# Two of VectorE's three power readings summed by accumulating DMAs in an attention and MLP kernel

## The chip, the cores and the metric

The kernel runs on one core of one Trainium2 chip. The core has five instruction queues: TensorE (PE in the profile; PEld are its weight loads), VectorE (DVE), ScalarE (ACT), GpSimd (POOL) and SyncE (SP), and 16 DMA engines that all queues share. The on-chip memories are SBUF and PSUM; PSUM has eight banks of 128 x 512 fp32. The metric is device time in microseconds, as the median of several runs; a profiled execution is recorded beside them.

## The reference

Two branches over the same 2048 tokens of width 640, mixed by a gate that is one number per token:

```python
qkv = (x @ wqkv).reshape(B, S, 3, H, Dh).transpose(2, 0, 3, 1, 4)   # S = 2048, H = 32, Dh = 20
scores = einsum("bhqd,bhkd->bhqk", q, k) * Dh ** -0.5
a = einsum("bhqk,bhkd->bhqd", softmax(scores), v).transpose(0, 2, 1, 3).reshape(B, S, D) @ wo

h = einsum("bsd,df->bsf", x, w1) + b1                             # F = 1536
b = einsum("bsf,fd->bsd", h * tanh(softplus(h)), w2)

g = sigmoid((x * gate_w).sum(-1, keepdims=True))
out = g * a + (1 - g) * b
```

Both branches read the same x. All matrices are bf16. The largest part is the softmax: 32 heads x 2048 x 2048 exponentials.

## The kernel before

**Groups, sets and units.** The attention is cut into 32 groups G: four heads (p) times 512 queries (qc). Within a group the 2048 keys are 16 blocks j of 128. The scores of one block and one head are a *unit*: 128 keys x 512 queries, one PSUM bank, one matmul with a 32-row tile (L1033, four heads in four row tiles). A whole block j of a group, four units, goes one of two ways:

- *ScalarE's way.* Steps S n,bank write n units into n neighbouring banks (`emit_s`); step x exponentiates them in one instruction into the ring E (`emit_exp`, L1051). Step V j,-1 multiplies the block with the values (`emit_pv`, L1068): four matmuls, one per head, 21 value columns each (20 and a column of ones, which gives the softmax's denominator), accumulated in bank 7.
- *VectorE's way, a "set".* Step d takes block j out of the group for VectorE and gives it a tile T of 128 x 2048 bf16. Steps D compute its four units, and for each a VectorE instruction (L556, `power_of`) multiplies and adds so that the result, taken as int16, is the bit pattern of a bf16 power of two with a linear mantissa. One such power is a coarse exponential. So further *readings* are made of it: GpSimd adds a constant to the bits (an INT64_ADD over the tile, L586, `add_shift`), which moves the place where the mantissa breaks, and the readings are added up.

**Readings before.** In 153 of 160 sets (`d_shifts`) there are three readings: T itself and two shifted copies, made by two INT64_ADDs (the last in place). All three go to TensorE: V j,0 with the values VA, V j,1 and V j,2 with values scaled by RATIO (VD, made per p by two VectorE instructions). That is three readings, 12 matmuls, for one set; the sum is made in PSUM. In 7 of 160 sets (`d_sum`) GpSimd shifts T into a second tile, VectorE adds T to it (L610), GpSimd then shifts T in place, and TensorE reads two tiles: the sum with VA, the shifted T with VD.

**The other work of the same engines.** Projections, the value matrix, the two MLP products and the output product are "chains": step C takes the next one with a bank, every step F runs one piece (four matmuls, L633), and at its end VectorE copies the bank out. VectorE also normalises each finished group (transpose L1097, reciprocal L1104, product L1111). ScalarE runs the MLP's activation in two long instructions (step m, L840). SyncE issues the loads and stores: per group four query rows (step q, L749), per p the keys (step k), stores of the normalised groups (L1144), the MLP's weights (L431) and its results.

**The order.** Nothing is scheduled while the kernel runs: every engine's queue follows `ORDER`, a recorded list of steps in order of time, that a loop runs through (`steps`). Step y n runs the n-th waiting VectorE instruction, p n,k the n-th waiting GpSimd step, with k the tile T that it may write (-1: in place). Each step appends to its engines' queues, which run in order; a wait in front of an instruction holds all that stands behind it on that engine. There are nine tags for tiles T (T0 to T8), 18 units in the ring E and seven banks for scores and chains. Step H is four matmuls with zero weights that keep TensorE busy.

Of the kernel before, what the change touches and what calls it, by code (L numbers as in the profile page):

```python
# [11 lines left out]
ALU = mybir.AluOpType  # L12
# [7 lines left out]
S2,0 S2,2 C1,6 F x C2,5 F y1 x C3,4 F y2 S2,0 y3 C4,6 F x S3,2 y4 C5,5 F F F F x F F F F F F F F F F F F S2,0  # L20
F F S3,2 x F F C0,6 F F y5 x y6 F y7 F y8 y9 F S2,0 y10 V0,-1 x V1,-1 V2,-1 C6,6 F F F F F V3,-1 C7,5 F y11
C8,4 F y12 S2,0 S2,2 q1 C9,6 F y13 x C10,5 F y14 C11,4 F F x F F y15 F S2,0 F F F F x F F F S2,2 F F F F x F
S2,0 S2,5 F F F x y16 C12,3 F y17 y18 F y19 F y20 F x S3,0 F V4,-1 x V5,-1 y21 V6,-1 C13,6 F S3,3 y22 C14,2 F
x S2,0 y23 C15,6 F C16,2 F x y24 S3,3 y25 V7,-1 C17,6 F x F F F F F F F F F S2,0 F F F F x F S3,2 F F F F F
C18,5 F x F y26 y27 F y28 S2,0 y29 y30 F F x S2,2 y31 V8,-1 V9,-1 x V10,-1 d1,0,1 S2,0 S2,4 d1,1,0 D1,15,0,6
d1,2,0 d1,3,0 x C19,3 F y32 F F F x S3,0 D1,15,3,6 F y33 V11,-1 x S2,4 y34 C20,6 F F F F F F F F F F F x F
S3,0 D1,14,0,3 F F F y35 F F x F F F S2,4 y36 C21,3 F y37 y38 F y39 y40 e0 F v0 y41 F x S3,0 D1,15,1,6 q2 y42
V12,-1 y43 F V13,-1 x V14,-1 y44 S2,4 D1,14,3,6 C22,3 F y45 F F x F S2,0 D1,15,2,2 V15,-1 y46 F x F F S2,4
D1,13,0,6 y47 F p1,4 F F x C23,2 F F y48 F S2,0 F y51 F x S2,4 D1,13,3,6 y52 F y49 F y50 F F F x V0,-1 S2,0
D1,14,1,3 V1,-1 y53 x p2,-1 V15,0 S2,4 y55 C24,6 F y56 x F y57 F S2,0 D1,14,2,2 y54 d1,4,0 F x S2,3 D1,12,0,5  # L30
y58 F V2,-1 y59 x V15,1 p3,5 S2,0 D1,13,1,2 y60 V3,-1 V14,0 x y61 p4,0 S2,3 D1,12,3,5 C25,6 V14,1 y62 F x S2,0
D1,13,2,2 d2,1,0 F y63 F x S3,3 F p5,5 F x V4,-1 S2,0 D1,12,2,2 y64 V14,2 V13,0 y65 V5,-1 p6,0 x V13,1 S3,3
D1,12,1,6 d2,5,0 V6,-1 y66 C26,2 F x F F V13,2 F S2,0 D1,11,0,6 p7,2 F F y67 F x F q3 S2,3 D1,11,1,5 p8,0
V12,0 y68 F F x S2,0 D1,11,3,6 V7,-1 y69 V12,1 y70 x V12,2 y71 S2,2 D1,11,2,5 D2,15,1,4 d2,0,0 V8,-1 y72 x
C27,6 F F S2,0 F y73 p9,2 F F x F S2,2 D2,15,2,5 F F y74 F p10,3 F x S2,0 D2,15,0,4 V11,0 y75 V9,-1 y76 x
V11,1 y77 S2,2 D2,14,1,6 D2,14,2,5 V11,2 y78 x V10,-1 S2,0 D2,15,3,4 d2,2,0 y80 C28,6 F x F S2,2 y79 V0,-1 x
y81 F S2,0 D2,14,0,5 F y82 p11,3 y83 F x S2,2 D2,13,1,4 V1,-1 y85 V15,0 p12,4 x S2,0 D2,14,3,5 y86 d2,6,0
V15,1 C29,6 F y87 x F S2,2 D2,13,2,4 V15,2 y84 F F x y88 p13,1 F S2,0 D2,13,0,5 F F y89 F x F S2,2 D2,12,1,4
p14,3 F V2,-1 y90 V14,0 x S2,0 D2,13,3,5 y91 d3,4,0 C30,4 F F y92 F x F y93 F S2,2 D2,12,2,6 F F y94 F x F
S2,0 D2,12,0,5 V3,-1 y95 F x V14,1 S2,2 D2,11,1,6 y96 p15,1 V14,2 y97 V4,-1 x y98 S2,0 D2,12,3,5 d3,3,0 V13,0  # L40
y99 V5,-1 x S3,2 D2,11,2,6 p16,-1 V13,1 y100 V6,-1 x V12,0 p17,1 S2,0 D2,11,0,5 V13,2 y101 C32,6 F F p18,0 x F
S3,2 D2,11,3,5 d3,5,0 F y102 x F V7,-1 V12,1 y103 S2,0 D3,15,1,5 p19,1 V12,2 y104 V8,-1 x S3,2 D3,15,0,6 V11,0
p20,0 y105 V11,1 x S2,0 D3,15,2,5 V9,-1 y106 C31,6 F F F x S3,2 D3,14,1,5 V11,2 y107 F x F S2,0 y108 V10,-1
C33,5 F F y109 x F S3,2 D3,14,2,6 F y110 y111 x F V0,-1 S2,0 y113 C34,6 F F F y112 F F x F S3,2 D3,15,3,5 q4
d3,0,0 F F y114 F x F V1,-1 V2,-1 y115 S2,0 D3,13,1,5 p21,1 y116 V15,0 y117 C35,6 F x F S3,2 k1 p22,2 F F F F
x F S2,0 D3,14,3,5 F F y118 F V15,1 V3,-1 x V15,2 y119 S3,2 D3,12,1,5 y120 V4,-1 v1 y121 C36,6 F x F F y122
# [36 lines left out]
S2,2 D8,13,1,6 x y261 V15,0 V2,-1 y262 V15,1 x p67,0 S2,0 D8,13,0,5 D8,13,3,4 V15,2 y259 y263 V3,-1 x V14,0
# [213 lines left out]
def kernel(  # L297
# [12 lines left out]
    nc = tc.nc  # L310
# [1030 lines left out]
```

## Time and profile before

| | |
|---|---|
| median of 3 runs | 697.11 us (696.96 to 699.27) |
| profiled execution, its own time | 697.02 us |
| its span, first to last instruction | 695.2 us |
| TensorE's granted clock | 0.998 |
| chain that ended last, shares | PE 78%, ACT 15%, DVE 3%, issue 3%, DMA 1% |
| L1068 on E, on T with VA, on T with VD | 133.9, 62.4, 117.4 us busy for 1408, 640, 1252 matmuls |
| DMA queue of SyncE and ScalarE (q1) | 38.38 MB, 24.7% of 16 engines' span |
| DMA, whole core | 40.46 MB, mean 58 GB/s |

The page gives for each engine how long it was busy, and for each group of instructions how long the engine stood idle before it and which engine's instruction ended that idle time. Matmuls overlap one another, so a TensorE that is busy is not necessarily at its peak, and a group's busy time is not the time that it would be shorter without it. DMA issues are not counted as busy time of the issuing engine.

### The profile page before, as it was taken

The page shows a single profiled execution, that of the slowest core. Times are in us where ns is not written, and L with a number is a line of the kernel's source. Part 1 is how long each engine was busy: PE and PEld are TensorE (multiplying, and loading weights), DVE is VectorE, ACT ScalarE, POOL GpSimd, SP SyncE. Part 2 cuts the span into 40 slices and gives each one's busy share as a digit, 9 for nine tenths or more (in the row PEclk, how much of TensorE's full clock was granted, in tenths as well). Part 3 has the DMA queues.
Part 4 walks back from the last instruction along what each step waited for, and adds up shares of the span by engine and source line. Part 5 has one row for each costly group of instructions (what it writes and reads, how often), then busy time and mean ns, then how long its engine had stood idle before and what let it go on. Part 6 is the DMA issues. An engine that isn't in the chain of part 4 may idle for free.

```text
span 695.2 us, 24441 instructions
## 1 busy us (share of the span) xinstructions
PE 680.5 (98%) x10325; PEld 240.0 (35%) x10325; DVE 582.0 (84%) x1009; ACT 676.6 (97%) x665; POOL 339.6 (49%) x334
## 2 busy tenths in 40 slices
PE   8999999999999999999999999999999999999997
PEld 4433333332323343333333222222234333343333
DVE  4488868888799888788898999988989988888896
ACT  5899999999999999999999999999999999999996
POOL 5025443435365434544547555554643565545543
PEclk9999999999999999999999999999999999999999
DMA  9612132313211212112031214232222121143221
GB/s 249 194 15 46 32 75 52 58 51 85 50 26 33 67 37 40 27 38 56 24 83 36 43 32 90 44 67 57 37 63 81 22 50 29 41 74 61 58 58 48
DMA packets 125613, 40.46 MB, mean 58 GB/s; under 512 B 91136, under 2 KB 124944, under 8 KB 125504
## 3 DMA queue, kind: packets, MB, share of 16 engines
q1 hardware_dynamic: 123904, 38.38, 24.7%
q8 instruction: 80, 1.31, 0.8%
q10 hardware_dynamic: 1600, 0.53, 0.3%
q14 instruction: 29, 0.24, 0.1%
HBM read 23.61 MB, written 12.79 MB: 52 GB/s over the span
## 4 chain that ended last, share of the span: by engine, by line
PE 78%; ACT 15%; DVE 3%; issue 3%; DMA 1%; SPq 0%; DVEq 0%; ACTq 0%
PE Sp L1033 26%; PE Sp L1068 26%; PE Sp L633 24%; ACT E L1051 11%; ACT big L840 3%; DVE T L556 2%; DMA w_top<-in_A_wqkv_dram 1%; PE Sp L1284 0%; ACT L1051 0%; PE Sp L1184 0%; DVE VD L538 0%; DVE big L819 0%; DVE T L1111 0%; PE Sp L643 0%; DVE bt L864 0%
## 5 line engine op out<-in xcount | busy, mean ns | idle before, releaser
L1051 ACT ACTIVATE E<-Sp 128x1024 bf16<-128x1024 f32 (+1 forms) x650 | 645.5, 1175 | 5.1 <-PE Sp L1033 4.0
L586 POOL INT64_ADD T<-T x320 | 330.4, 1043 | 340.6 <-DVE T L556 195.8
L556 DVE TENSOR_SCALAR T<-Sp 128x512 int16<-128x512 f32 x640 | 425.0, 685 | 76.9 <-PE Sp L1033 67.3
L1033 PE MATMUL Sp<-qT,kT 32*128 32x512 bf16 x2048 | 260.4, 383 | 6.2 <-ACT E L1051 3.0
L1033 PEld LDWEIGHTS <-kT 32*128 32x128 bf16 x2048 | 71.5, 91 | 240.5 <-issue 236.0
L1068 PE MATMUL Sp<-E,VA 128*21 128x512 bf16 x1408 | 133.9, 383 | 0.0
L1068 PE MATMUL Sp<-T,VD 128*21 128x512 bf16 x1252 | 117.4, 382 | 0.2
L633 PE MATMUL Sp<-w_sb,big 128*32 128x320 bf16 x1536 | 74.2, 301 | 0.6 <-DVE T L556 0.5
L633 PE MATMUL Sp<-xT,w1t 128*32 128x512 bf16 x960 | 73.4, 383 | 0.2
L1068 PEld LDWEIGHTS <-VA 128*21 128x21 bf16 x2048 | 45.5, 90 | 63.3 <-issue 54.2
L1068 PE MATMUL Sp<-T,VA 128*21 128x512 bf16 x640 | 62.4, 381 | 0.0
L633 PE MATMUL Sp<-xT,ws 128*32 128x512 bf16 x720 | 52.3, 381 | 0.2 <-ACT E L1051 0.2
L633 PEld LDWEIGHTS <-big 128*32 128x32 bf16 x1536 | 35.0, 95 | 28.0 <-issue 19.6
L1068 PEld LDWEIGHTS <-VD 128*21 128x21 bf16 x1252 | 30.8, 90 | 39.1 <-issue 32.7
L819 DVE TENSOR_SCALAR big<-Sp,b1f 128x512 bf16<-128x512 f32 x48 | 35.6, 741 | 1.5 <-PE Sp L633 1.1
L633 PE MATMUL Sp<-wv,xT 128*32 128x81 bf16 (+2 forms) x960 | 33.3, 257 | 0.4 <-DVE st L721 0.2
L633 PE MATMUL Sp<-wo_sb,od 128*32 128x320 bf16 (+1 forms) x608 | 28.9, 301 | 0.6 <-DVE T L556 0.6
L633 PEld LDWEIGHTS <-w1t 128*32 128x32 bf16 x960 | 20.1, 95 | 26.3 <-issue 19.4
L721 DVE CAST st<-Sp 128x512 bf16<-128x512 f32 x36 | 24.7, 685 | 5.3 <-PE Sp L633 5.2
L633 PEld LDWEIGHTS <-xT 128*32 128x32 bf16 x960 | 19.1, 96 | 12.8 <-issue 9.2
L777 DVE CAST VA<-Sp 128x80 bf16<-128x80 f32 (+2 forms) x48 | 16.2, 373 | 8.2 <-PE Sp L633 8.2
L633 PEld LDWEIGHTS <-ws 128*32 128x32 bf16 x720 | 16.8, 95 | 17.7 <-issue 10.0
(75 smaller groups left out, 206.1 us busy)
## 6 DMA issues: line engine op xcount, KB each, us to landing
w1t<-in_B_w_dram SPq DMA_DIRECT2D x24, 320.0 KB
q_dram<-st SPq DMA_DIRECT2D x20, 128.0 KB
b_dram<-bt SPq DMA_DIRECT2D x16, 160.0 KB
bl<-b_dram SPq DMA_DIRECT2D x16, 160.0 KB
out_dram<-ot SPq DMA_DIRECT2D x16, 160.0 KB
qT<-q_dram SPq DMA_DIRECT2D x124, 20.0 KB
o_dram<-T SPq DMA_DIRECT2D x120, 20.0 KB
kT<-k_dram SPq DMA_DIRECT2D x28, 80.0 KB
```

The source lines that it names most:

```text
L556: nc.vector.tensor_scalar(out=dst.bitcast(I16), in0=src, scalar1=inv_sqrt_dh * LOG2E * 128.0, scalar2=127.0 * 128.0 + (BETA2 if two else B ...
L586: nc.gpsimd.int64_add(dst[:, :].bitcast(I64), src[:, :].bitcast(I64), n * 0x0001000100010001)
L633: nc.tensor.matmul(out_[k : k + 32], lhsT=lhsT[:, k : k + 32], rhs=rhs, tile_position=(0, k), **kw)
L721: nc.vector.tensor_copy(out=res["st"][:, :], in_=ps[:, :])
L777: nc.vector.tensor_copy(out=VA[:, sts[i], h0 : h0 + nh, 0:DH], in_=ps[:, i, 0:n].rearrange("p (h d) -> p h d", d=DH),)
L819: nc.vector.tensor_scalar(out=big[:, pair_of(c, ft), (ft % 2) * QC : (ft % 2 + 1) * QC], in0=ps[:, :], scalar1=b1f[:, ft : ft + 1], scalar ...
L840: nc.scalar.activation(v, v, ACT.Mish)
L1033: nc.tensor.matmul(ps_cols, lhsT=kT[p][32 * t_ : 32 * t_ + 32, j * P : (j + 1) * P], rhs=qT[G][32 * t_ : 32 * t_ + 32, :], tile_position=( ...
L1051: nc.scalar.activation(E[:, x : x + n, :], allb[:, k0 : k0 + n, :], ACT.Exp, scale=inv_sqrt_dh,)
L1068: nc.tensor.matmul(acc[32 * t_ : 32 * t_ + DH + 1, :], lhsT=lhsT, rhs=rhs, start=(pv_done[G] == 0), stop=(pv_done[G] == pv_total[G] - 1), ...
```

## The change

`d_sum`'s sum is no longer a VectorE instruction. GpSimd issues a DMA instead, from T to the shifted tile, that adds to its destination; it is queued as one more GpSimd step, and the second shift follows as a step after it:

```diff
         def shift(k):
             d[0] = t_tile(k)
             add_shift(d[0], d["T"], SHIFT2[0])
-            dve(total, lambda: gps(again))
-
-        def total():
-            nc.vector.tensor_tensor(out=d[0][:, :], in0=d[0][:, :], in1=d["T"][:, :], op=ALU.add)
+            gps(total)
+
+        def total(k):
+            nc.gpsimd.dma_start(out=d[0][:, :], in_=d["T"][:, :], accum_op=ALU.add)
+            gps(again)
 
         def again(k):
             d[1] = d["T"]
             add_shift(d[1], d["T"], SHIFT2[1])
```

The DMA waits for the first shift; the second shift and the reading V j,0 wait for the DMA. In the order, p n,-2 is the step that issues it.

`ORDER` is replaced as a whole. What the two lists hold:

| steps | before | after |
|---|---|---|
| sets (d) | 160 | 172 |
| of them summed to two readings | 7 (by VectorE) | 151 (by DMA) |
| units on VectorE (D) | 640 | 688 |
| blocks of scores and exponentials (S, x) | 650 | 668 |
| of 1, 2, 3 units | 0, 542, 108 | 1, 642, 25 |
| units on ScalarE | 1408 | 1360 |
| readings (V): of E, first, second, third | 352, 160, 160, 153 | 340, 172, 172, 21 |
| readings in all | 825 | 705 |
| VectorE instructions by step y | 975 | 1016 |
| GpSimd steps p: shifts, DMA issues | 320, 0 | 344, 151 |
| chains, pieces (C, F) | 191, 1223 | 191, 1223 |
| heating (H) | 3 | 9 |
| loads q, k, b, o; m | 31, 7, 16, 8; 2 | 31, 7, 16, 8; 2 |

The order's texture changes with it. A stretch from before and one from after; the DMA issue p n,-2 stands between a set's first shift (p n,k) and its second (p n,-1), with other sets' steps between:

```diff
-y505 V12,0 x V13,1 y508 p152,2 S2,0 D16,11,2,6 d17,5,0 V3,-1 y509 C110,5 F p153,-1 F x F S3,2 D16,10,0,6 F
...
+x y550 p253,-1 V12,1 S2,2 D17,13,0,6 D17,13,3,5 V7,-1 x y551 S2,0 D17,14,2,4 p256,3 d17,4,1 V8,-1 y552 V11,1 x
+C113,6 F F y553 p258,-2 S2,2 D17,12,0,5 F x y554 S2,0 D17,13,1,4 p259,5 F y555 F x V9,-1 S2,2 D17,12,3,5 y556
+p261,-2 C114,4 F F x y557 S2,0 D17,13,2,6 d17,7,1 F p257,-1 y558 F x S2,2 D17,11,0,5 V10,0 y559 F x S2,0
```

More of the change, by code (lines that the diff above doesn't have):

```diff
@@ L25 @@
[L25 to L34, printed above, removed]
@@ L280 @@
[L280 to L283 removed]
+S2,0 S2,2 C1,6 F x C2,5 F y1 C3,4 F x y2 S2,0 C4,6 F y3 x S3,2 y4 C5,5 F F F F F x F F F F F F F F F F F F F F
@@ new lines @@
+d5,8,1 F x y176 F S2,2 D5,13,1,5 p62,-2 F y177 x V8,-1 S2,0 D5,13,0,4 p58,-1 V12,0 y178 C45,5 F x F F y179
+S2,2 D5,13,2,6 p63,7 F F x y180 S2,0 D5,13,3,4 V9,-1 y181 p65,-2 V12,1 x C46,6 F y182 S2,2 D5,12,1,5 d5,4,1 F
+p61,-1 y183 x F S2,0 D5,12,0,4 F y184 x F S2,2 D5,12,2,5 V11,0 y185 p64,-1 V10,-1 x S2,0 D5,12,3,4 y186 d5,2,1
+V11,1 C47,6 F y187 x S2,2 D5,11,1,5 p67,3 F y188 F x S2,0 D5,11,0,4 y189 p69,-2 F F y191 x V15,0 S2,2
+D5,11,2,5 p66,-1 y192 V14,0 x V0,-1 S2,0 D5,11,3,4 y193 d6,0,1 V15,1 p68,7 V1,-1 y194 x S2,2 D5,10,1,6
@@ new lines @@
+D5,10,2,5 V2,-1 y190 p72,5 y195 V14,1 x S2,0 D5,10,0,4 V3,-1 y196 C48,6 F p71,-2 x F y198 S2,2 D6,15,1,5 F
+y197 x F S2,0 D5,10,3,4 y199 p73,-2 d6,1,1 F x V4,-1 y200 S2,2 D6,15,2,5 V13,0 p70,-1 y201 V5,-1 x S2,0
+D6,15,0,4 y202 C50,6 F p76,3 F x F F y203 F S2,2 D6,14,1,5 V13,1 y204 p77,-2 x S2,0 D6,15,3,4 y205 d6,6,1
+C57,6 V6,-1 F y206 x F S2,2 D6,14,2,5 p74,-1 V12,0 y207 F x q7 S2,0 D6,14,0,4 q8 F p79,7 y208 F x S2,2
+D6,13,1,5 q9 V11,0 y209 p75,-1 V7,-1 x S2,0 D6,14,3,4 y210 d6,5,1 V12,1 p80,-2 V8,-1 y211 x V11,1 S2,2
@@ new lines @@
+V12,1 S2,2 D9,10,3,5 d10,1,0 C72,6 F p137,-1 y325 x V13,1 V6,-1 S2,0 D10,15,0,4 F p139,-2 y326 x S2,2
+D10,15,2,5 F y327 V12,2 p140,0 x F S2,0 D10,15,1,4 F y328 V7,-1 x p142,-2 S2,2 C73,5 F y329 F F x S2,0
+D10,14,0,4 F V8,-1 y330 x F S2,2 y331 D10,15,3,6 d10,3,1 C74,4 F x y332 F S2,0 D10,14,1,5 F p144,6 x y333
+V9,-1 S2,2 D10,14,2,6 F y334 x V11,0 p141,-1 S2,0 D10,13,0,5 F y335 C75,6 F x p145,-2 F S2,2 y336 D10,14,3,5
+d10,5,1 F x p143,-1 y337 S2,0 D10,13,1,4 F y338 x V10,0 S2,2 D10,13,2,5 F y339 V11,1 x S2,0 V10,1 y340 C77,5 F
@@ new lines @@
+x S2,2 D19,15,0,4 V13,2 y602 p285,7 F x S2,0 D19,15,2,5 k5 V5,-1 k6 y603 F x p284,-2 S2,2 D19,15,1,4 V6,-1
+y604 C122,5 F x F p286,-2 y605 S2,0 D19,15,3,6 v5 d19,0,1 F y607 x F S2,2 D19,14,0,4 y606 p283,-1 F V12,0 x
+y609 S2,0 D19,14,2,6 V7,-1 p289,3 y610 V12,1 x S2,2 D19,14,1,4 y611 V8,-1 p290,-2 C123,5 F x F y612 S2,0
+D19,14,3,6 d19,8,1 F y608 x F y613 S2,2 D19,13,0,4 p287,-1 F y614 x V11,0 S2,0 D19,13,2,6 V9,-1 y615 p288,-1
+V10,0 x S2,2 D19,13,1,4 y616 V11,1 p292,5 C124,5 F y617 x S2,0 D19,13,3,6 d19,2,1 V10,1 y618 F x S2,2
@@ new lines @@
+S2,2 D21,14,1,5 q24 V7,-1 y675 x V11,0 S2,0 D21,14,3,6 p319,-1 y676 d21,6,0 V8,-1 C132,4 F x y677 S2,2
+D21,13,0,5 F y678 F x p325,7 S2,0 D21,13,2,6 F y679 F x p321,-1 S2,2 D21,13,1,5 V10,0 y680 V9,-1 x S2,0
+D21,13,3,6 y681 p326,-2 d21,8,0 V11,1 V10,1 y682 x C133,5 F S2,2 D21,12,0,4 y683 d22,0,0 F p328,2 x F y684
+S2,0 D21,12,2,6 F p324,-1 y685 V15,0 x y686 S2,2 D21,12,1,4 d22,4,0 V0,-1 y687 V1,-1 x S2,0 D21,12,3,6 y688
+p329,-2 F V2,-1 x y689 S2,2 D21,11,0,4 V15,1 y690 V3,-1 x C134,6 F S2,0 y691 D21,11,1,5 p327,-1 V14,0 x y692
@@ new lines @@
+V15,0 C152,6 F x y816 p387,-1 F S2,2 F y817 V14,0 x S2,0 D25,10,3,5 p388,-1 F V2,-1 y818 x V15,1 S2,2
+D25,11,2,4 p391,5 d26,0,1 F V3,-1 y819 x S2,0 D26,15,0,5 p390,-1 V13,0 y820 b5 V14,1 x y821 C155,4 F S2,2
+D25,10,1,6 p392,-2 F F y822 o1,0,4 x F S2,0 D26,15,3,5 F p393,1 V4,-1 y823 x V13,1 S2,2 D25,10,2,6 y824
+d26,3,1 C153,5 F p395,-2 F y825 x F F S2,0 D26,14,0,4 F V5,-1 p397,6 y826 x S2,2 D26,15,1,6 F V6,-1 y827 x F
+S2,0 D26,14,3,4 p398,-2 F F y828 x F S2,2 D26,15,2,6 d26,7,1 F V7,-1 y829 x F p394,-1 S2,0 D26,13,0,4 y830
@@ new lines @@
+p441,-1 F F y914 x F S2,2 D29,15,3,5 p446,-2 d29,0,1 F F y915 F x S2,0 D29,14,1,6 F F y916 F x F S2,2
+D29,14,0,5 y917 V12,0 V6,-1 x y918 S2,0 D29,14,2,6 D29,13,1,4 p448,2 V12,1 y919 V11,0 x S2,2 D29,14,3,5
+p444,-1 d29,3,1 V7,-1 y920 V8,-1 x D29,13,0,6 y921 S2,0 D29,13,2,4 p449,-2 V9,-1 y922 x V11,1 S2,2 D29,13,3,5
+y923 p450,5 d29,7,1 C172,6 F F x V10,0 y924 S2,0 D29,12,1,4 F p447,-1 F y925 x F S2,2 D29,12,0,5 y926 b10
+C173,4 F p452,-2 F x y927 F S2,0 D29,12,2,6 V10,1 p453,6 y928 x F S2,2 D29,12,3,5 d30,8,1 F y929 F F x F
@@ new lines @@
+p455,-2 S2,0 D29,11,1,6 y930 V0,-1 F y932 x S2,2 D29,11,0,5 p451,-1 F y931 F y933 F x V15,0 S2,0 D29,11,2,6
+y935 p457,2 V1,-1 y934 x V2,-1 S2,2 D29,11,3,5 D30,15,0,4 V3,-1 V15,1 x y936 p458,-2 S2,0 d30,4,1 V14,0 y937
+V4,-1 x S2,2 D30,15,3,6 p454,-1 y938 C176,5 F F x F F y939 S2,0 D30,15,1,4 p460,5 F F y940 x F F S2,2
+D30,14,0,6 p456,-1 F F x y941 S2,0 D30,15,2,4 F p461,-2 F y942 V13,0 x o2,4,5 o3,0,3 S2,2 D30,14,3,6 y943
+d30,6,1 V5,-1 V14,1 y944 x S2,0 D30,14,1,5 D30,14,2,4 p463,1 V6,-1 y945 V12,0 x V13,1 S2,2 D30,13,0,6 y946
@@ L284 @@
+V3,-1 x p488,-1 S2,2 D31,10,3,6 y1001 V14,1 y1002 C186,4 F x S2,0 D31,10,1,5 p489,1 F y1000 F F x F S2,2
+D31,9,0,6 y1003 p490,2 V4,-1 V12,1 y1004 x S2,0 D31,10,2,5 y1005 p491,3 V11,0 V12,2 x S2,2 D31,9,3,4 y1006
+V5,-1 y1007 V11,1 p492,0 x V11,2 S2,0 D31,9,1,6 D31,9,2,5 V6,-1 y1008 x V10,0 p493,1 V10,1 S2,2 y1009 C187,6 F
+F x F F p494,0 S1,0 y1010 V7,-1 x V10,2 V9,0 p495,2 V9,1 V8,-1 C188,6 F F F F C189,5 F V9,2 y1011 F F F y1012
+C190,4 F F F F y1013 y1014 y1015 y1016
 """
```

485 lines of the change are left out of this document (232 added, 253 removed).

## The prediction

> **What bounds the kernel now.** I read the header first, then the busy time by stages, then the groups of instructions kept apart by shape, then single pieces of the timeline. The header (PE is TensorE, PEld its weight loads, DVE VectorE, ACT ScalarE, POOL GpSimd):
>
> ```profile
> span 695.2 us, 24441 instructions
> PE 680.5 (98%) x10325; PEld 240.0 (35%) x10325; DVE 582.0 (84%) x1009; ACT 676.6 (97%) x665; POOL 339.6 (49%) x334
> ```
>
> Two engines at 97 and 98% of a mean over unequal stages; so the stages (columns: start:end, length, busy us of PE, PEld, DVE, ACT, POOL with instructions, then TensorE's clock, DMA share, GB/s):
>
> ```profile
> 0.00:25.00 25.00, 20.88 (x344) 11.42 (x348) 11.12 (x42) 16.05 (x18) 9.23 (x14) 1.00 0.97 257
> 300.00:400.00 100.00, 99.86 (x1483) 32.45 (x1483) 87.52 (x145) 99.93 (x102) 55.46 (x54) 1.00 0.20 45
> 400.00:500.00 100.00, 99.66 (x1316) 28.35 (x1316) 90.68 (x152) 99.93 (x104) 55.12 (x55) 1.00 0.27 57
> ```
>
> From 300 to 500 us ScalarE is never idle (99.93) and TensorE hardly ever; VectorE has 9 to 12 us in 100 free, GpSimd 45. So two engines set the pace together, and a gain needs less work on both. The groups (last columns: busy us, mean ns of one, idle before them):
>
> ```profile
> L1051 ACT ACTIVATE E<-Sp 128x1024 bf16<-128x1024 f32 x542 | 521.6, 1102 | 4.6 <-PE Sp L1033 3.7 <-ACT E L1051 0.2
> L556 DVE TENSOR_SCALAR T<-Sp 128x512 int16<-128x512 f32 x640 | 425.0, 685 | 76.9 <-PE Sp L1033 67.3 <-POOL T L586 1.3 <-issue 0.2
> L586 POOL INT64_ADD T<-T x320 | 330.4, 1043 | 340.6 <-DVE T L556 195.8 <-PE Sp L1068 62.9 <-PE Sp L1033 33.6
> L1051 ACT ACTIVATE E<-Sp 128x1536 bf16<-128x1536 f32 x108 | 166.6, 1543 | 0.5 <-PE Sp L1033 0.4
> ...
> L610 DVE TENSOR_TENSOR T<-T 128x2048 bf16<-128x2048 bf16 x7 | 8.5, 1207 | 0.6 <-POOL T L586 0.6
> ```
>
> The exponentials (L1051) are 645.5 us of ScalarE's 676.6 (the two shapes overlap, so their busy times add to more). GpSimd waits for work: 340.6 us idle before its shifts. TensorE's true price of one reading, four matmuls of L1068, is the distance between starts, 0.22 us, since the matmuls overlap:
>
> ```profile
> 676.72 0.40 PE L1068 MATMUL Sp<-T,VD 128*21 128x512 bf16 x4
> ...
> 676.94 0.39 PE L1068 MATMUL Sp<-E,VA 128*21 128x512 bf16 x4
> ...
> 677.16 0.31 PE L633 MATMUL Sp<-wo_sb,od 128*32 128x320 bf16 x4
> ```
>
> **The change part by part.** Counts are from the two recorded orders.
>
> *ScalarE.* Score units of 512 columns exponentiated fall from 1408 to 1360, in 668 instructions (642 of two units, 25 of three, 1 of one) for 650 (542 and 108). Three units last 1543 - 1102 = 441 ns longer than two. With a for the two-unit step, 542a + 108(a + 0.441) = 645.5 gives a = 0.920 us. After: 642 x 0.920 + 25 x 1.361 + 0.48 = 625.1. Saved: 20.4 us, on the path.
>
> *TensorE.* Readings fall from 825 to 705: 120 x 0.22 = 26.4 us less. Heating steps rise from 3 to 9 (1.3 us), and 18 more blocks of scores each switch the shape once more; a block of three or four scores takes 0.32 to 0.33 us in the chain of waits against 0.22 for a reading, so about 0.11 each, 2 us. Net 23 us less, a little more than ScalarE saves: TensorE does not become the bound.
>
> *VectorE.* 48 more powers (688 for 640) at 425.0/640 = 0.664 us are 31.9 us; the seven sums of L610 go, 8.5. So 582.0 + 23.4 = 605.4, 90% of a 675 us span. In dense stages it is nearly full: in the order's stretch that answers to 400 to 500 us the powers rise from 106 to 114, and 90.7 + 5.3 = 96 us stand in a stage shortened to about 97.
>
> *GpSimd.* Two INT64_ADD a set for 172 sets: 344 for 320, 25 us more. New are 151 DMA issues. No row shows one. Below: SyncE's issue rows, median 482 ns for the stores of o_dram; above: twice an INT64_ADD, 2.08 us. I take one INT64_ADD, 1.04: the row nearest in engine and operand size, and between the two ends. Then 339.6 + 25 + 157 = 522 us, 77% of the span. A set costs 2.08 + 1.04 = 3.1 us against one set in about 3.7 (172 sets in some 640 us): it fits, with 0.6 to spare.
>
> *The accumulating DMA's time.* It replaces a wait inside the engines by one on a transfer of 128 x 2048 x 2 B = 524 KB. Behind it waits GpSimd's own second shift (it overwrites the source), and behind that, in GpSimd's order, the next sets' shifts and issues; TensorE's reading V j,0 waits for the same DMA. From the rows: in the first 25 us the DMA engines were 97% busy at 257 GB/s, so one pass of 524 KB is 2.04 us, two passes (source and destination both read) 4.08. The fixed part: the last store of 160 KB is issued by
>
> ```profile
> 691.86 0.89 SPq L1310 DMA_DIRECT2D out_dram<-ot  x2
> ```
>
> so by 692.75, and the span ends at 695.2: 2.45 us, less 0.64 for the bytes, 1.8. Lower end 1.8 + 2.04 = 3.8 us; upper end 1.8 + 4.08 stretched by the other queue's 24.7% share, 1.8 + 5.4 = 7.2; the issue comes on top. The order puts 6 to 8 exponentials between issue and second shift in 146 of 151 sets (most often 7), at 625.1/668 = 0.94 us or more: 6.6 us. The first reading stands behind 6 or more too. Up to 7.2 + 1.04 = 8.2 against 6.6: most of the interval is covered. I take 5.5 us with issue, near the middle, where nothing waits.
>
> [...]
>
> *SyncE's queue.* Its loads and stores keep their kinds and counts; the order leads each group's query load by 10 or more exponentials (before, two stood at 1 and 4), which covers a load delayed by a summing DMA. Cost nothing; without that cover, one 0.5 to 3 us stall for each of 31 loads. Tiles T stay longer in use (a source is held for about seven exponentials more), all within the nine tiles; a late DMA also frees them late, and then VectorE's next power, its bank, and TensorE's next score are late.
>
> *Sum.* The profiled execution took 697.02 us, 1.8 outside its span, and the median is 697.11. 697.0 - 20.4 = 676.6. After the last exponential the order has 5 readings and 12 pieces of product where it had 3 and 6; two readings (0.4) and six pieces at about 0.17 make 1.4 us more tail. **678 us.**
>
> **The rivals.**
>
> *Slower: the DMAs set the pace.* Up to three are in flight: from one issue to the third after it lie its completion and three INT64_ADD on GpSimd, so three sets take at least L + 3.1 us, where the order wants 3 x 3.7 = 11.1. L up to 8.0 is free; beyond it each microsecond costs 151/3 = 50 us. At L = 8.4 the gain is gone; at 9, 151 x (12.1/3 - 3.7) = 50 us: 728. For it: three in flight share the same engines with 24.7% of other traffic, and if each kept the engines busy for 4.08 us, 151 x 4.08 + 172 = 788 us of DMA time would not fit in 676 at all. Against: that rate is one of loads from HBM in short pieces, and here rows are 4 KB within SBUF.
>
> *Slower: GpSimd's issue.* Above 1.6 us an issue, GpSimd sets the pace: at 2.08, 151 x 0.46 = 69: 747. For it: 340.6 us of idle before becomes little. Against: an issue on SyncE's queue takes a quarter of that, and the only GpSimd rows above 1.3 us are two startup memsets of 1.8 and one of 2.4.
>
> *VectorE becomes the bound.* Full in the middle stages, it passes each small wait on to ScalarE: with 2% of the 500 us from 100 to 600, 10 us: 688. For it: the 96 of 97 us; against: ScalarE and TensorE both ran at over 99% before.
>
> *No change: VectorE holds up GpSimd's issues.* If each issue had to wait out one L556 of 0.69 us, a set would cost GpSimd 3.8 us for 3.7 and 151 x 0.11 = 17 us would be lost: 695. Against: INT64_ADD runs at 1032 to 1264 ns, median 1040, beside a VectorE that is 84% busy. [...]
>
> That the change does not do what it says is excluded: 151 issues stand in the order.
>
> **How the numbers follow.** The plan holds, about 672 to 684: 40%. VectorE the bound: 18%. VectorE holding up issues: 6%. DMAs set the pace: 25%. The issue: 11%. About half a per cent is what a measurement of this kernel tells from no change (3.5 us). Faster 0.58, same 0.06, slower 0.36. The range runs from 669 (ScalarE's saving plus the other engines' small idle) to 732, which takes in the DMA rival at L = 9 and leaves its extreme and the issue's out; the likeliest case's own range is 672 to 684.
>
> **What would show it.** ScalarE's busy time near 656 us and above 99% from 100 to 500; L1068 with 120 x 4 matmuls fewer; VectorE near 605; 151 DMAs of 512 KB on a new queue, GpSimd's second shift rarely waiting for one, TensorE's readings of T never. The forecast is wrong if GpSimd's waits for DMAs come to over 100 us together with ScalarE idle before L1051, or if GpSimd is busy or issuing over 95% of the middle.

## The result and the profile after

The changed kernel takes 746.63 us (median of 3 runs, 739.35 to 746.68), where the kernel before takes 697.11 (696.96 to 699.27): a ratio of 1.067, 95% interval 1.056 to 1.077. It is slower by 49.5 us, where 678 us was forecast, and outside the range of 669 to 732. The profiled execution took 746.63 us, its span is 744.8 and TensorE's granted clock 0.967.

The header, the DMA queues and the first line of the chain that ended last:

```profile
span 744.8 us, 23800 instructions
...
PE 690.0 (93%) x9869; PEld 229.6 (31%) x9869; DVE 610.3 (82%) x1050; ACT 667.0 (90%) x683; POOL 495.9 (67%) x509
...
q0 software_dynamic: 21744, 79.18, 56.7%
q1 hardware_dynamic: 123904, 38.38, 24.1%
...
PE 44%; DMA 30%; POOL 10%; DVE 8%; issue 4%; SPq 2%; ACT 2%; ACTq 0%; DVEq 0%; POOLq 0%
```

No engine is full any more: ScalarE falls from 97 to 90% and TensorE from 98 to 93%. The new queue q0 holds the 151 sums: their packets took 56.7% of the span of all 16 DMA engines, and DMA, 1% of the chain before, is 30% of it. The groups (busy us, mean ns of one, idle before it and what ended that):

```profile
L1069 ACT ACTIVATE E<-Sp 128x1024 bf16<-128x1024 f32 (+1 forms) x668 | 635.9, 1076 | 61.9 <-PE Sp L1051 59.2
L573 DVE TENSOR_SCALAR T<-Sp 128x512 int16<-128x512 f32 x688 | 453.7, 683 | 96.8 <-PE Sp L1051 82.3
...
L627 POOL DMA_DIRECT2D T<-T x151 | 134.1, 898 | 22.8 <-POOL T L603 21.1
...
L1086 PE MATMUL Sp<-T,VA 128*21 128x512 bf16 x688 | 67.7, 390 | 31.3 <-DMA T<-T 30.8
L651 PE MATMUL Sp<-xT,w1t 128*32 128x512 bf16 x960 | 81.9, 397 | 5.3 <-DMA w1t<-in_B_w_dram 5.0
```

L1069, L1051, L1086, L651 and L603 are the exponential, the scores, the readings, the chains and the shift. ScalarE's idle time before an exponential grows from some 5 to 61.9 us, ended by scores; the scores stand in TensorE's queue behind readings of T (L1086), which wait 30.8 us for summing DMAs, and behind chains that wait for weights which SyncE loads (L651). GpSimd waits too, as the list of waits shows (waiting line, releaser, us, times, longest):

```profile
POOL T L603 <- DMA T<-T: 73.9, 55, 5.6
ACT E L1069 <- PE Sp L1051: 59.2, 62, 3.7
PE Sp L1086 <- DMA T<-T: 30.8, 28, 3.0
```

The stages say when (columns as before; the last three are the clock, the DMA share and GB/s):

```profile
150.00:200.00 50.00, 44.49 (x557) 12.66 (x554) 39.82 (x65) 39.90 (x42) 31.84 (x33) 0.91 0.93 179
...
300.00:350.00 50.00, 47.91 (x707) 15.76 (x704) 41.93 (x71) 47.19 (x51) 40.43 (x42) 0.97 0.97 184
...
500.00:550.00 50.00, 47.76 (x618) 14.91 (x610) 46.73 (x73) 47.99 (x41) 34.80 (x35) 1.00 0.48 85
...
650.00:700.00 50.00, 47.23 (x710) 15.82 (x707) 43.84 (x74) 46.18 (x50) 39.82 (x41) 0.96 1.05 186
```

From 300 to 500 us the DMA share was 0.20 to 0.27 before; in three of these stages it is 0.93 to 1.05, and from 50 to 700 us as a whole 0.85: the engines are full in stretches, not throughout. (A share is the time that packets took; over 1, as the 1.05 here, their times overlap.) One stretch in slices of 5 us shows the sequence:

```profile
170.00:175.00 5.00, 4.53 (x61) 1.21 (x53) 4.89 (x8) 4.87 (x6) 3.16 (x5) 1.00 1.07 229
175.00:180.00 5.00, 3.24 (x44) 0.91 (x40) 3.94 (x7) 3.77 (x4) 3.57 (x4) 1.00 1.01 209
180.00:185.00 5.00, 4.11 (x60) 1.49 (x60) 3.72 (x7) 3.87 (x4) 3.33 (x4) 1.00 1.10 217
185.00:190.00 5.00, 2.98 (x26) 0.68 (x27) 1.92 (x4) 1.23 (x3) 3.47 (x4) 0.64 0.93 183
190.00:195.00 5.00, 5.00 (x52) 1.13 (x48) 3.20 (x5) 3.60 (x4) 2.01 (x2) 0.68 0.70 112
```

The timeline of that stretch (start, us, engine; in brackets the wait before it):

```profile
175.21 0.40 SPq L448 DMA_DIRECT2D w1t<-in_B_w_dram  x1
...
180.30 0.40 PE L1086 MATMUL Sp<-T,VA 128*21 128x512 bf16 x4 [2.06 <-DMA T<-T]
...
184.53 0.40 PE L1086 MATMUL Sp<-T,VA 128*21 128x512 bf16 x4 [0.59 <-DMA T<-T]
184.85 0.39 PE L1051 MATMUL Sp<-qT,kT 32*128 32x512 bf16 x3
187.26 1.90 PE L651 MATMUL Sp<-xT,w1t 128*32 128x512 bf16 x16 [2.02 <-DMA w1t<-in_B_w_dram]
...
189.63 0.61 PE L1086 MATMUL Sp<-T,VA 128*21 128x512 bf16 x4
```

The DMA engines are full; a reading waits 2.06 us for its sum; a load of 320 KB issued at 175.21 is there at 187.26, after 12 us, as the chain that ended last has it (start, us):

```profile
175.21 12.01 DMA w1t<-in_B_w_dram
```

TensorE stands for it from 185.24 to 187.26. Then the same group of matmuls shows 0.61 us for 0.40. In slices of 1 us (columns as above) the clock is halved for 6.8 us, from 186.4 to 193.2:

```profile
185.00:186.00 1.00, 0.24 (x3) 0.00 (x0) 0.73 (x3) 0.66 (x2) 1.00 (x2) 1.00 1.05 214
186.00:187.00 1.00, 0.00 (x0) 0.00 (x0) 0.97 (x2) 0.37 (x1) 0.62 (x1) 0.70 0.91 217
187.00:188.00 1.00, 0.73 (x8) 0.30 (x12) 0.00 (x0) 0.00 (x0) 0.83 (x1) 0.50 0.88 193
...
192.00:193.00 1.00, 1.00 (x11) 0.10 (x3) 0.64 (x1) 0.33 (x1) 0.00 (x0) 0.50 0.80 133
193.00:194.00 1.00, 1.00 (x14) 0.32 (x15) 0.71 (x2) 0.75 (x1) 0.00 (x0) 0.89 0.26 22
```

The wait of 2.06 us before 180.30 was as long, and the clock stayed at 1.00 in the slices around it. The wait of 2.02 us came 0.7 us after another one, of 0.59. So the length of a single wait does not settle whether the clock falls.

### The profile page after: what moved, and what is told of

Same layout as the page of the kernel before. It is cut to its first block, busy times and chain, and to the rows that moved or that the text cites. A ratio compares the mean times of both kernels' runs of the same rounds, so it can differ in the third digit from the quotient of the medians.

```text
span 744.8 us, 23800 instructions
## 1 busy us (share of the span) xinstructions
PE 690.0 (93%) x9869; PEld 229.6 (31%) x9869; DVE 610.3 (82%) x1050; ACT 667.0 (90%) x683; POOL 495.9 (67%) x509
## 3 DMA queue, kind: packets, MB, share of 16 engines
q0 software_dynamic: 21744, 79.18, 56.7%
q1 hardware_dynamic: 123904, 38.38, 24.1%
## 4 chain that ended last, share of the span: by engine, by line
PE 44%; DMA 30%; POOL 10%; DVE 8%; issue 4%; SPq 2%; ACT 2%; ACTq 0%; DVEq 0%; POOLq 0%
DMA T<-T 23%; PE Sp L1051 16%; PE Sp L651 15%; PE Sp L1086 13%; POOL T L603 8%; DVE T L573 4%; DMA w1t<-in_B_w_dram 3%; POOL T L627 2%; ACT E L1069 2%; DMA w_sb<-in_B_w_dram 1%; DVE T L1129 1%; DMA o_dram<-T 1%; DMA wf<-in_A_wqkv_dram 1%; SPq L448 1%; DMA od<-o_dram 1%
## 5 line engine op out<-in xcount | busy, mean ns | idle before, releaser
L1069 ACT ACTIVATE E<-Sp 128x1024 bf16<-128x1024 f32 (+1 forms) x668 | 635.9, 1076 | 61.9 <-PE Sp L1051 59.2
L573 DVE TENSOR_SCALAR T<-Sp 128x512 int16<-128x512 f32 x688 | 453.7, 683 | 96.8 <-PE Sp L1051 82.3
L603 POOL INT64_ADD T<-T x344 | 377.4, 1126 | 209.2 <-DVE T L573 93.0
L1051 PE MATMUL Sp<-qT,kT 32*128 32x512 bf16 x2048 | 278.6, 393 | 8.5 <-DVE T L573 2.9
L627 POOL DMA_DIRECT2D T<-T x151 | 134.1, 898 | 22.8 <-POOL T L603 21.1
L1051 PEld LDWEIGHTS <-kT 32*128 32x128 bf16 x2048 | 71.2, 91 | 250.7 <-issue 243.6
L1086 PE MATMUL Sp<-E,VA 128*21 128x512 bf16 x1360 | 130.5, 392 | 0.0
L1086 PE MATMUL Sp<-T,VA 128*21 128x512 bf16 x688 | 67.7, 390 | 31.3 <-DMA T<-T 30.8
L651 PE MATMUL Sp<-xT,w1t 128*32 128x512 bf16 x960 | 81.9, 397 | 5.3 <-DMA w1t<-in_B_w_dram 5.0
L651 PE MATMUL Sp<-w_sb,big 128*32 128x320 bf16 x1536 | 80.8, 310 | 0.0
L1086 PEld LDWEIGHTS <-VA 128*21 128x21 bf16 x2048 | 47.5, 91 | 104.5 <-issue 83.7
L1086 PE MATMUL Sp<-T,VD 128*21 128x512 bf16 x772 | 77.9, 397 | 0.5 <-POOL T L603 0.4
L651 PE MATMUL Sp<-xT,ws 128*32 128x512 bf16 x720 | 55.3, 385 | 0.0
L651 PEld LDWEIGHTS <-big 128*32 128x32 bf16 x1536 | 34.5, 97 | 30.5 <-issue 22.9
L651 PE MATMUL Sp<-wo_sb,od 128*32 128x320 bf16 (+1 forms) x608 | 32.7, 312 | 1.8 <-DMA od<-o_dram 1.8
L651 PE MATMUL Sp<-wv,xT 128*32 128x81 bf16 (+2 forms) x960 | 32.8, 262 | 0.2 <-DVE T L573 0.2
L651 PEld LDWEIGHTS <-w1t 128*32 128x32 bf16 x960 | 21.0, 95 | 35.4 <-issue 25.9
L1086 PEld LDWEIGHTS <-VD 128*21 128x21 bf16 x772 | 20.4, 91 | 27.6 <-issue 24.9
L1129 DVE TENSOR_TENSOR T<-T,rec 128x320 bf16<-128x320 f32 x31 | 23.9, 771 | 0.1
L651 PEld LDWEIGHTS <-xT 128*32 128x32 bf16 x960 | 19.7, 99 | 13.5 <-issue 10.8
```

Source lines behind the costliest of these rows:

```text
L573: nc.vector.tensor_scalar(out=dst.bitcast(I16), in0=src, scalar1=inv_sqrt_dh * LOG2E * 128.0, scalar2=127.0 * 128.0 + (BETA2 if two else B ...
L603: nc.gpsimd.int64_add(dst[:, :].bitcast(I64), src[:, :].bitcast(I64), n * 0x0001000100010001)
L627: nc.gpsimd.dma_start(out=d[0][:, :], in_=d["T"][:, :], accum_op=ALU.add)
L651: nc.tensor.matmul(out_[k : k + 32], lhsT=lhsT[:, k : k + 32], rhs=rhs, tile_position=(0, k), **kw)
L1051: nc.tensor.matmul(ps_cols, lhsT=kT[p][32 * t_ : 32 * t_ + 32, j * P : (j + 1) * P], rhs=qT[G][32 * t_ : 32 * t_ + 32, :], tile_position=( ...
L1069: nc.scalar.activation(E[:, x : x + n, :], allb[:, k0 : k0 + n, :], ACT.Exp, scale=inv_sqrt_dh,)
```

## The experiments

Ten kernels, each timed beside the kernel before, whose median there was 697.2 to 697.4 us. They take apart three things: the new order, GpSimd's issue of a DMA, and the bytes that the DMA engines move.

**1. The order alone.** The line of the DMA is left out; the sum is not made.

```diff
-            nc.gpsimd.dma_start(out=d[0][:, :], in_=d["T"][:, :], accum_op=ALU.add)
```

> The summing DMA is left out, nothing in its place: the first reading of 151 sets holds the shifted power alone, so the output is not the reference's; the order and all other instructions stay. Three theories of the 746.6 us: (A) the summing DMAs take the 16 DMA engines, so that sums and loads land late, and TensorE's clock falls as a consequence of the stalls; (B) GpSimd's queue sets the pace, with the issue (0.9 us) and the wait for each DMA in front of the second shift; (C) the new order is slower by itself, for instance because VectorE is full. A and B: 676 to 684 us, clock back at 0.99 or more. C: above 700.

685.97 us, ratio 0.984 (0.983 to 0.985): 2 us above the range of theories A and B, and far from the 700 of C. Its header, and two stretches of it:

```profile
span 685.6 us, 23603 instructions
...
PE 669.9 (98%) x9869; PEld 228.2 (33%) x9869; DVE 602.0 (88%) x1050; ACT 658.2 (96%) x683; POOL 366.1 (53%) x358
```

```profile
25.00:50.00 25.00, 20.70 (x383) 8.85 (x382) 14.76 (x36) 17.65 (x19) 3.10 (x3) 0.85 0.22 65
...
300.00:400.00 100.00, 99.73 (x1446) 31.52 (x1434) 93.34 (x155) 99.81 (x109) 58.69 (x57) 1.00 0.23 48
```

The first of these stretches in the kernel before:

```profile
25.00:50.00 25.00, 23.64 (x470) 10.37 (x470) 16.64 (x41) 24.74 (x25) 2.08 (x2) 1.00 0.23 60
```

So the order by itself gains 11.4 us, and the sums cost 60.6 (746.6 - 686.0). The two spans split that cost: 744.8 - 685.6 = 59.2 us, of which TensorE's busy time, for the same 9869 matmuls, is 20.1 (690.0 - 669.9, with a granted clock of 0.967 for 0.991) and time in which it does nothing 39.1. The readings' waits for sums, 30.8 us, are the largest part of that. From 300 to 400 us ScalarE and TensorE run at over 99%, as forecast. That 686.0 is not 678 comes in part from the start: from 25 to 50 us ScalarE is busy for 17.65 us and was for 24.74 before, with a clock of 0.85 for 1.00. The timeline there:

```profile
24.10 6.28 SPq L705 DMA_DIRECT2D k_dram<-kT  x8
...
30.48 0.35 SPq L741 DMA_DIRECT2D q_dram<-st  x1
33.74 1.39 SPq L766 DMA_DIRECT2D qT<-q_dram  x4
...
35.65 0.60 PE L1050 MATMUL Sp<-qT,kT 32*128 32x512 bf16 x1 [2.50 <-DMA qT<-q_dram]
```

Group 1's queries are loaded behind eight stores of keys and a store of queries in SyncE's queue; TensorE waits 2.5 us for them and then runs matmuls of 0.60 us, at a clock of 0.54 from 35 to 40 us.

**2. That load.** As 1, with group 1's query rows taken from x, which is there from the start (that group's scores are not the reference's).

```diff
-                in_=q_dram[r0 : r0 + DH, qc * QC : (qc + 1) * QC],
+                in_=(x2d[r0 : r0 + DH, 0:QC] if G == 1 else
+                     q_dram[r0 : r0 + DH, qc * QC : (qc + 1) * QC]),
```

> No sums, and the second group's query rows are loaded from the input x instead of from the stored projection (the output is not the reference's), so that this one load needs not wait for the store in front of it in SyncE's queue. Theory of the order's shortfall (686.0 without sums where 678 was forecast): TensorE waited 5.3 us for this load at about 31 to 36 us, and its clock stood at 0.66 for the next 10 us. Then 677 to 681. If VectorE's fullness in the middle is the reason, 684 to 687, unchanged.

682.63 us, 0.979 (0.977 to 0.981): 3.3 us of the 8, a miss. (The 5.3 us of the expectation are that wait of 2.5 and, once more, the 2.8 for which the weight loads of the same matmuls waited.) The load no longer waits for its store, but it stands behind the same key stores in SyncE's queue, and TensorE still waits 1.3 us, with a clock of 0.87 from 25 to 50 us. The load accounts for 3.3 us; the rest was not taken apart further, beyond a tail of 11.0 us after the last exponential (674.59 to 685.6) where the kernel before has 8.5.

**3. The issue without the bytes.** The sum is made for 64 of the 2048 columns.

```diff
-            nc.gpsimd.dma_start(out=d[0][:, :], in_=d["T"][:, :], accum_op=ALU.add)
+            nc.gpsimd.dma_start(out=d[0][:, 0:64], in_=d["T"][:, 0:64], accum_op=ALU.add)
```

> The DMA sums 64 of 2048 columns, 16 KB for 512 KB: issue, completion and every wait stay, the bytes go (the output is not the reference's). A: 678 to 692 us, the new queue's share of the DMA engines below 15%. B: 725 or more, since GpSimd still issues 151 times and still waits. C: above 700 in any case.

696.21 us, 0.998 (0.996 to 1.000): 10.2 us more than without the DMA, 4 above the range of theory A and far under the 725 of B. In its groups, the issue and the normalising product of VectorE:

```profile
L627 POOL DMA_DIRECT2D T<-T x151 | 133.9, 895 | 22.9 <-POOL T L603 21.4
...
L1129 DVE TENSOR_TENSOR T<-T,rec 128x320 bf16<-128x320 f32 x31 | 32.7, 1055 | 0.1
```

and the same product in experiment 1:

```profile
L1128 DVE TENSOR_TENSOR T<-T,rec 128x320 bf16<-128x320 f32 x31 | 20.3, 654 | 0.1
```

An issue takes 0.877 us at the median, well under the 1.6 from which GpSimd would set the pace. But VectorE's busy time is 615.6 for 602.0, and 12.4 of the 13.6 us are that product. Of its instances some that lie beside an issue are long (up to 2.55 us) and some are not (0.51), and one of 3.37 lies beside none; what lengthens them is not settled.

**4. The bytes without the addition.** The same 512 KB, copied.

```diff
-            nc.gpsimd.dma_start(out=d[0][:, :], in_=d["T"][:, :], accum_op=ALU.add)
+            nc.gpsimd.dma_start(out=d[0][:, :], in_=d["T"][:, :])
```

> The DMA copies T over the shifted tile and does not add: same bytes, same issue, one source less to read (the output is not the reference's). A: between the two, 690 to 720, with the engines' share for this queue well below the 56.7% of the summing kernel. B: 735 or more, as the queue on GpSimd is the same.

691.70 us, 0.992 (0.990 to 0.993). Its queue on the page:

```profile
q0 software_dynamic: 21744, 79.18, 31.7%
```

its time from issue to landing, in the view of the tile T:

```profile
DMA to landing us min/median/max: 2.8/3.8/9.5
```

and the same line of the changed kernel:

```profile
DMA to landing us min/median/max: 4.4/6.0/10.0
```

The same packets and bytes take 31.7% of a span of 690.6 us: 1.45 us of all 16 engines each. The sums take 56.7% of 744.8: 2.80 each, 1.93 times as much. What the factor comes from, no run shows. Copies at this rate leave the engines some room (0.60 to 0.69 from 300 to 400 us), and the time is 0.8% under the kernel before.

**5. Half the columns**, added.

```diff
+            nc.gpsimd.dma_start(out=d[0][:, 0:1024], in_=d["T"][:, 0:1024], accum_op=ALU.add)
```

> The DMA sums 1024 of 2048 columns (the output is not the reference's). By theory A, with the summing pass as the cost (2.80 us of all 16 engines a DMA in the changed kernel, 1.45 for a plain copy, 0.32 for 64 columns), half the columns take about 1.5 us and 31% of the engines, like the plain copy, and the time is 693 to 705 us. If instead the adding itself sets the pace whatever the bytes, 710 or more.

697.76 us, 1.001 (0.999 to 1.003), with 33.1% on q0, 1.53 us each. From 64 to 1024 columns the time rises by 1.6 us, from 1024 to 2048 by 49. A cost for each byte would be a straight line; this is a knee.

**6. Less other traffic.** The sums are whole; w1 is loaded twice and not 24 times, so that most chains use an old block of it.

```diff
+            if k >= 2:
+                w1t[k] = w1t[k - 2]
+                return
```

> The summing DMAs stay; the first MLP weights are loaded twice and used again instead of 24 times (7.0 MB less on SyncE's queue; the output is not the reference's). A: 720 to 738 us, because 11 us of TensorE's waits for these loads go and the sums land sooner. B: 744 to 749, unchanged.

739.78 us, 1.059 (1.052 to 1.066), with q1 at 20.8% for 24.1%: a miss, just above the 720 to 738 forecast. The 7 us under the changed kernel are not clear of noise: its runs go from 733.71 to 744.08 us, those of the changed kernel from 739.35 to 746.68. The waits for w1 are gone, 5.0 us of TensorE's time (the 11 us of the expectation add those of its weight loads, mostly for the same stretches); the sums are nearly as late as before (5.7 us at the median).

**7. More patience.** A recorded order in which V j,0, V j,1 and the second shift of 149 sets come four exponentials later. It needs 12 tiles T; to make room, w2 is held as one block that all products use.

```diff
-    w2_sb = consts.tile([P, FT, D], BF16, tag="w2_sb")
+    w2_sb = consts.tile([P, 1, D], BF16, tag="w2_sb")
```

> Whole sums; in the order the first and last readings of 149 summed sets and their second shifts stand 4 exponentials later (8 to 14 behind the issue instead of 6 to 9), with 12 tiles T for 9; to make room the second MLP weights are one block of 128 rows instead of 12 (the output is not the reference's). Two forms of theory A: (A1) single DMAs land late, up to 10.0 us for a median of 6.0, while the engines have room on the whole: 4 exponentials are 3.8 us more patience, and the time falls to 690 to 705. (A2) the engines have no room left in the dense stages (shares of 0.92 to 1.05 in the windows), so that patience only moves the wait: 725 or more.

756.62 us, 1.086 (1.083 to 1.089). Its control, the same order with the DMA left out:

> The control for the later readings: the same order and tiles without the DMA (the output is not the reference's). Both forms: 684 to 692 us, as for the order of the changed kernel without it (686.0).

712.52 us, 1.022 (1.020 to 1.023), where 684 to 692 was expected: the order itself costs 26.5 us more than that of experiment 1, so the comparison is with this control. Within it the sums cost 44.1 us, though hardly anything waits for them any more. Two waits of the kernel with the sums:

```profile
ACT E L1069 <- PE Sp L1051: 61.0, 74, 2.9
...
POOL T L603 <- DMA T<-T: 7.2, 4, 3.1
```

GpSimd's wait for sums falls from 73.9 to 7.2 us, TensorE's from 30.8 to 1.0, and ScalarE stands for 61.0 us all the same (20.7 in the control). If a late sum were the whole matter, the loss would have gone; 44.1 us, for 60.6 in the order of the change, stay. Half of the difference of the two spans (41.4 us) is again the same matmuls at a lower clock (0.972, and 0.997 in the control): TensorE is busy for 697.8 us, and for 676.5 in the control. Of the 20.1 us in which it does nothing beyond the control, 9.3 are waits for loads of w1 and of the output product's operand, which the control does not have, and 7.3 are longer waits for GpSimd's shifts.

**8. Every second sum.** 76 whole sums instead of 151; the other sets go without their second term.

```diff
+            nsum[0] += 1
+            if nsum[0] % 2:
+                nc.gpsimd.dma_start(out=d[0][:, :], in_=d["T"][:, :], accum_op=ALU.add)
```

> The summing DMA is left out in every second of the 151 sets (those sets' first tile stays without its second term); the 76 that remain are whole, 512 KB each. Theory A, the 16 DMA engines are full: 76 adds at 2.80 us of the engines are 213 us, about 30% of the span, beside some 25% of the other queue; that is the load of the plain copy, so nearly all of the 60.6 us go: 689 to 698 us, a summing DMA lands in a median of 3.5 to 4.5 us, GpSimd waits under 20 us for them. Theory B, each summing DMA by itself takes longer than its set can wait (6.0 us at the median), whatever the others do: half the loss stays, 686.0 + 30 = 716 us, the median landing stays above 5 us, GpSimd waits 35 us or more.

701.23 us (696.17 to 704.81), 1.005 (1.001 to 1.008); its queue on the page, and the landing in the view of the tile T:

```profile
q0 software_dynamic: 10944, 39.85, 30.8%
```

```profile
DMA to landing us min/median/max: 4.4/5.2/9.3
```

15 of the 60.6 us stay, where a load limit asked for 3 to 12 and a limit of each sum by itself for 30. So the time came out nearer to A, and just outside its range; landing and GpSimd's wait came out as B said. A sum still needs 4.4 us at the least and 5.2 at the median, and GpSimd waits 41 us for the 76, so lateness has a part that is there at half the load too; but half of the sums cost a quarter of the loss. Each still takes 2.82 us of the engines (30.8% of 696.0 over 76): that figure is the sum's own and does not fall when there is less crowding.

**9. The load without the addition.** The plain copy, and a second copy of 512 KB to a scratch in DRAM that nobody waits for.

```diff
-            nc.gpsimd.dma_start(out=d[0][:, :], in_=d["T"][:, :], accum_op=ALU.add)
+            nc.gpsimd.dma_start(out=d[0][:, :], in_=d["T"][:, :])
+            nc.gpsimd.dma_start(out=s_dram[nsum[0]], in_=w2_sb.rearrange("p a b -> p (a b)")[:, 0:QC * 4])
+            nsum[0] += 1
```

> Each sum is replaced by two copies without an addition, both issued by GpSimd: the plain copy of the source tile onto the first tile, and a copy of 512 KB of the second layer's weights from SBUF to a DRAM scratch that nobody reads or waits for (the sums are left out). The DMA engines get about the load of the sums (twice 1.45 us a set, if the second copy costs what the first does), but nothing waits for the second copy. Theory A, the load of the engines is the cause: queue share near 55 to 60%, the shares by stage near 1, SyncE's loads and the first copies late, 730 to 755 us. Theory C, the addition is what is slow (an add holds up its own readers, other traffic is not touched): the time of one copy, 691.7, plus the second issue at 0.55 us on a GpSimd that has room: 692 to 702 us.

755.18 us, 1.082 (1.079 to 1.084), at the upper end of theory A and far from C.

```profile
PE 690.2 (92%) x9869; PEld 228.0 (30%) x9869; DVE 611.6 (81%) x1050; ACT 664.4 (88%) x683; POOL 524.4 (70%) x660
...
q0 software_dynamic: 43488, 158.35, 57.5%
```

Its stages:

```profile
300.00:350.00 50.00, 49.01 (x742) 16.40 (x741) 43.99 (x75) 49.01 (x53) 46.17 (x60) 1.00 0.99 335
...
600.00:650.00 50.00, 40.68 (x587) 13.02 (x583) 31.14 (x53) 36.44 (x39) 32.40 (x42) 0.84 0.90 264
```

What TensorE waits for in it:

```profile
PE Sp L1091 <- DMA T<-T: 16.3, 12, 3.7
...
PE Sp L656 <- DMA w1t<-in_B_w_dram: 12.0, 3, 6.3
```

Nothing is added here, and the loss of the changed kernel is there all the same: the q0 share (57.5 for 56.7%), TensorE's busy time (690.2 for 690.0), the full stages and the fallen clock (0.959 for 0.967). A copy takes 1.43 us of the engines, as in experiment 4, although the second one goes to DRAM. The waits differ: TensorE's for what GpSimd's DMAs write are shorter in sum (16.3 us for 30.8), those for w1 longer (12.0 for 5.0). In the same full stage, 300 to 350 us, the engines move 335 GB/s here and 184 with the sums: here bytes do not measure their load, time does. That stage shows another thing: at a share of 0.99 TensorE and ScalarE are both busy for 49.01 of 50 us, while from 600 to 650 us, at 0.90, they stand for 9 and 14. So a full stage does not cost time by itself. By the waits, what costs is a transfer that an engine stands for, and the runs do not show what decides which ones come late.

**One table.** A set comes every 3.7 us by the forecast's own count, and the other traffic takes 0.25 of the DMA engines (q1's 24.7% before; 0.21 in experiment 6). So the share that a kernel asks for is the engine time of a DMA over 3.7, plus 0.25:

| kernel | engine us per set | asked for | us |
|---|---|---|---|
| no DMA | 0 | 0.25 | 686.0 |
| 64 columns added | 0.32 | 0.34 | 696.2 |
| 512 KB copied | 1.45 | 0.64 | 691.7 |
| half added | 1.53 | 0.66 | 697.8 |
| every second sum | 2.82 / 2 | 0.63 | 701.2 |
| whole sums, w1 twice | 2.81 | 0.97 | 739.8 |
| whole sums (the change) | 2.80 | 1.01 | 746.6 |
| two copies | 2.87 | 1.03 | 755.2 |

(The engine time is q0's share of the span over the number of sets.) Up to 0.66 all lie between 1.6% under and 0.5% over the kernel before; from 0.97 on all lose 6 to 8%. Against the order without a DMA (686.0) the four kernels with one up to 0.66 cost 6 to 15 us, the last three 54 to 69. No kernel was run between. No version that computes everything and beats the kernel before came out: experiment 8 leaves half the sums out for nothing, and making up for them with a third reading would, by an estimate with the forecast's price of a reading, cost a full TensorE 75 x 0.22 = 16.5 us on top.

## Why the prediction was wrong

**The step that failed** is "The accumulating DMA's time". It took the DMA as a delay that the order must cover: 5.5 us with issue against 6.6 us of patience, "where nothing waits". The middle of that delay was not far off (6.0 at the median, inside its 3.8 to 7.2 and issue), but the longest took 10.0 us, and there were waits: 30.8 us of TensorE's readings and 73.9 of GpSimd. What it left out is that each sum also occupies the engines, for 2.80 us, and that 151 of them at one in 3.7 us beside a quarter of other traffic ask for 1.01 of what there is. Experiment 9 shows that such a load gives the loss without any addition; experiment 7, that more patience takes away the waits for sums and not most of the loss.

**The rival that came near** is "the DMAs set the pace", at 25%, by the wrong half of itself. It was priced by its rule of three in flight, free up to 8.0 us; at a median of 6.0 that rule gives no loss at all. Its other sentence, that at 4.08 us each the DMA time "would not fit in 676 at all", is near the mechanism: the load of the engines. It was set aside because that rate came from loads of HBM in short pieces, and no rate was put in its place. Even with the true 2.80 its sum would have fitted, 151 x 2.80 + 172 = 595 of 676 us, 88%: a mean over the span, which includes the start, the end and the thin stage from 500 to 550 us (share 0.48). At the planned pace the dense stages ask for all of it. The forecast warned of such means for the engines and then used one for the DMAs.

**SyncE's queue, "cost nothing".** Wrong, by two ways. A lead of ten exponentials did not help a load that stands behind stores in SyncE's queue (group 1's, for which TensorE waits 2.5 us in experiment 1), and with the engines as full as here the loads of weights and products are late as well: TensorE waits 5.0 us for w1 and 1.8 for the output product's operand in the changed kernel, and 12.0 for w1 in experiment 9. The price named for lost cover, 0.5 to 3 us a load, was the author's estimate, with no row behind it; in the changed kernel the matmuls' single waits for DMAs are 3.0 us at the longest.

**What was not foreseen: the clock.** 20.1 of the 59.2 us of span are the same matmuls at a lower clock (0.967 for 0.991). In the stretch shown it fell within a wait of 2.02 us, 0.7 us behind one of 0.59, and stayed at 0.50 for 6.8 us, in which groups of matmuls took 0.61 us for 0.40; in a wait of 2.06 us shortly before, and after it, it stayed at 1.00. So there slow matmuls came on top of the wait; what decides whether they come, the runs do not show.

**The terms that held.** *ScalarE*: forecast 656, in experiment 1 658.2, and over 99% busy from 300 to 500 us, so that neither *TensorE* nor *VectorE* holds it up there; VectorE's busy time is 602.0 us without the DMA and 610.3 with it, for 605.4 forecast. *GpSimd*: 0.874 us an issue at the median for 1.04 taken, 495.9 us in all for 522 (its issues, 134.1 us, are counted as busy here); the rival that its issue sets the pace has no support. *VectorE holding up issues* has no support here: an issue took 0.874 us at the median and 1.43 at the most. It was the other way round if anything: VectorE's product of two SBUF operands is longer in the kernels with issues (1055 ns in experiment 3 and 771 in the changed kernel, for 654 in experiment 1). The issues with their side effects are worth about 10 us there, a term that the forecast did not have. *Tail*: 2.5 us more for 1.4.

**By its own tests**: over 100 us of waits of GpSimd for DMAs, with ScalarE idle before its exponentials, were to prove it wrong. GpSimd's are 73.9, and TensorE's readings, which were to wait never, add 30.8; ScalarE's idle time came as named.

Where the shortfall of experiment 1 lies, ScalarE's rows tell. Its profiled execution took 687.42 us, 9.4 above the forecast: 2.0 are busy time (658.2 for 656.2), 6.3 idle time before exponentials (11.4 us, for 5.1 in the kernel before), and 1.1 the tail. Open stay what makes up the idle time beyond the late load of group 1, what lengthens VectorE's product, how much of the 15 us of experiment 8 is the sums' lateness, and why some full stages lose time and others do not.

## What to carry to other kernels

A sum by DMA had two prices here: the delay from issue to landing (6.0 us at the median), which an order could cover (in experiment 7 GpSimd's waits for sums fell from 73.9 to 7.2 us), and the time that it holds the DMA engines (2.80 us), which more patience in the order did not give back (44.1 us of loss stayed). Divide the second by the interval between such DMAs in the densest stage, add the share of all other traffic there, and keep the sum well below 1 (here 0.63 to 0.66 cost 6 to 15 us, 0.97 and more 54 to 69). Work that is moved from a compute engine to the DMA engines shares them with the loads: here TensorE, 98% busy before and with no wait for w1, waits 5.0 us for it after the change, and one load of it took 12.0 us.

## What the runs showed of the hardware

- An accumulating DMA of 512 KB within SBUF takes 2.80 us of all 16 engines, a copy of the same bytes 1.45; landing 4.4 and 2.8 us at the least.
- GpSimd issues the adding form in 0.874 us and the copy in 0.547 (medians), and for the adding form the size hardly matters: 0.877 for 64 columns, 0.874 for 1024.
- A small add cost the kernel more than a large copy: 696.2 us with 64 columns added, 691.7 with 512 KB copied.
- Within a wait of TensorE of 2.02 us, 0.7 us behind one of 0.59, its clock fell to 0.50, for 6.8 us; in one of 2.06 us, and after it, it stayed at 1.00.
